# Four interleaved attention layers on one core: another row table for a unit of ten phases, with four shared maxima in place of three, and exp tiles picked by which engine last read the product's bank

## The chip, the cores and the metric

One core of a Trainium2 chip runs the whole kernel. The metric is the device time of one execution in microseconds (us), lower is better. Before the change the median of three runs is 5589.08 us (5588.31 to 5590.57).

## The reference, cut to what matters

Four transformer layers follow each other on `x` of 2048 tokens by 576 channels: attention A, attention B, A again, B again, each with a layer norm ahead and a residual sum behind it. There are 32 heads of 18 channels. In B all heads share one key and one value.

```python
def layer_A(x):                       # x: 2048 x 576, after the layer norm
    q, k, v = split(x @ wqkv)         # 32 heads of 18 channels
    scores = einsum("hqd,hkd->hqk", q, k) * 18 ** -0.5
    p = softmax(scores, axis=-1)
    return einsum("hqk,hkd->hqd", p, v).reshape(2048, 576) @ wo

def layer_B(x):                       # the same, with one k and one v for all heads
    q, k, v = x @ wq, x @ wk, x @ wv
    ...

x = x + layer_A(layernorm(x)); x = x + layer_B(layernorm(x))
x = x + layer_A(layernorm(x)); x = x + layer_B(layernorm(x))
```

## The kernel before, in words

**What a layer does.** It projects q, k and v, then works through 16 pairs of heads (`p`) and four blocks of 512 queries (`u`): 64 units of work in a layer. Head 0 of the pair (`a` = 0) has its rows in partitions 0 to 63 of the `big` tile, head 1 in partitions 64 to 127, so a product of one head uses one half of TensorE's rows.

**What a unit does.** Three kinds of step run interleaved, for different units:

- *Maxima.* 32 steps `m`: a product of 128 queries by 512 keys (`psm`, lines 593), of which VectorE takes the row maximum (`reduce_max`, line 598). With a *shared* maximum, two blocks of keys of the same queries are covered by one step `r` and one step `m`: `r` is the product with the difference of the two key blocks (line 587), of which ScalarE takes the Relu (line 591); the later `m` is the ordinary product of the first block, and VectorE's `tensor_tensor_reduce` (line 596) adds the Relu to it and takes the maximum of the sum. So each `r` puts one more instruction on ScalarE and one less on VectorE.
- *Exponentials.* 32 steps `e` (`exp_mm`): a product of 128 keys by 512 queries (`pse`, line 812), then Exp on ScalarE into an SBUF tile `pt` (line 816). The maxima of that unit were found 14 steps (`LEAD`) earlier, and go through `neg` (line 788), GpSimd, a transpose on VectorE (line 797) and DRAM into rows of `big`.
- *Weighted sums.* `pv_cols` and `pv_block`: four products at a time (line 837) of `pt` tiles with v, into the four column groups of the one bank `oacc`. They lag the exponentials by 928 columns (`PV_LAG`). When a unit is done ScalarE copies `oacc` out as `oc` (line 844), and GpSimd sums and scales it (`o_sum`, `o_mul`).

**What sets the order.** The order is written by hand. The table `UNIT` lists ten phases, each a string of rows and a number of columns. A row is a kind (`m`, `r` or `e`), a head and a rank: `e01` is an exponential of head 0 of rank 1. The loop at the end issues a phase's rows and then as many columns of weighted sums. All engines take their instructions in that order.

**Banks.** PSUM has eight banks: `oacc` and seven that the rows share. `lru` lists the seven by how long ago each was handed out; a row takes the one at its rank (0 is the oldest), so its product waits until ScalarE or VectorE has read what that bank held before.

**Exp tiles.** `ptile` hands out 15 SBUF tiles in turn, for `pt`, `oc` and others. An Exp that writes a tile which ScalarE wrote earlier may need a wait of ScalarE on its own semaphore, where no other wait implies it. `run_todo` issues the small steps of the other units (loads, sums, the path of the maxima) at the start of a phase.

**Names of the phases.** Counted 0 to 9 in table order. A phase's *score part* is the time from its first row's product to its first weighted sum; its *sum part* goes from there to the next phase's first product.

Of the kernel before, what the change touches and what calls it, by code (L numbers as in the profile page):

```python
# [64 lines left out]
UNIT = [("e01 m10 e00 m10 m00 e11", 384),  # L65
        ("m10 e00 m10 e00 e10 m01", 544),
        ("e10 m01 e10 m01 m10 e00", 384),
        ("e10 m00 e10 e00 m10 e01", 352),
        ("m10 m00 e10 m00 e01 r10", 416),
        ("m00 e10 r11 e00 m11 e00 m10", 416),  # L70
        ("m01 e10 e10 e11 m00 e01 m10", 384),
        ("m10 e00 m00 e11 m00 e11", 384),
        ("m00 r10 e00 m01 e10 m01 e10", 416),
        ("m11 e00 e00 m00 e10 e00 m10", 416)]
# [7 lines left out]
def tile_kernel(ctx: ExitStack, tc: tile.TileContext, A_x, A_wqkv, A_wo, B_x, B_wq, B_wk, B_wv, B_wo, out):  # L82
# [65 lines left out]

    lru, turns = list(range(7)), {"m": 0, "e": 0}
# [260 lines left out]
    for layer in range(4):  # L410
# [125 lines left out]
        def ops(p):  # L536
            return big[:, q_slot(p)], big[:, k_slot(p)]
# [35 lines left out]
        def max_mm(bank=mtile):  # L573

            i = m_done[0]
# [5 lines left out]
            mx, ps = mxs[p, u], bank("psm")  # L581
            b, r = 64 * a, 16 * a + 4 * qc + kb
            c0 = u * 512 + qc * P
            if (p, u) >= (0, 2) and (a, qc, kb) in m_diff:
# [5 lines left out]
                t = relus[p, u, a, qc] = relu[:, :512]  # L590
                nc.scalar.activation(t, ps, AF.Relu)  # L591
# [16 lines left out]
        relus, diffs, kd_pair = {}, {}, {}  # L608

# [196 lines left out]
        def exp_mm(p, u, i, rank):  # L806

            a, kc = (i // 2) % 2, i // 4 * 2 + i % 2
            q, k = ops(p)
            e = oldest(rank)("pse")  # L810
            r = 64 * a
            nc.tensor.matmul(e, k[r:r + KE, kc * P:(kc + 1) * P], q[r:r + KE, u * 512:(u + 1) * 512],  # L812
                             start=True, stop=True)

            pt = pts[p, u, i] = ptile("pt")
            nc.scalar.activation(pt, e, AF.Exp, scale=SCALE)  # L816

# [11 lines left out]
        def pv_block(n, c0, c1):  # L829
# [4 lines left out]
            for i in range(i, i + 4) if turn[0] % 2 else range(i + 3, i - 1, -1):  # L834
                a, kc = (i // 2) % 2, i // 4 * 2 + i % 2
                j = 64 * a + 32 * (kc % 2)
                nc.tensor.matmul(oacc[j:j + DH + 1, cs], v_of(kc)[:, 2 * p + a if is_a else 0, :], pts[p, u, i][:, cs],  # L837
                                 start=kc < 2 and c0 == 0, stop=kc >= 14 and c1 == 512)
                if c1 == 512:
                    pts.pop((p, u, i))  # L840
            if c1 == 512 and i // 4 == STEPS - 1:
                oc = ocs[p, u] = ptile("oc")
# [92 lines left out]
        e_next = [0, 0]  # L935

# [65 lines left out]
```

## Time and profile before

| | before |
|---|---|
| time, median of 3 | 5589.08 us |
| the profiled execution: its time, its span | 5593.45 us, 5591.6 us |
| busy share of the span, TensorE / VectorE / ScalarE / GpSimd | 99 / 89 / 87 / 33% |
| TensorE's granted clock | 0.998 |
| rows per layer in the loop over `UNIT` | 1992 of 2048 `m` and `r` |

"PE" is TensorE's products, "PEld" its weight loads, DVE is VectorE, ACT ScalarE, POOL GpSimd, SP the queue that issues DMAs. A row of the timeline reads: start, duration, engine, line, operation, output and input, how many of them in a run. The start and end of an instruction on ACT and DVE overlap with the next one's: their rate is read from one start to the next, not from the duration. Ends of products are modelled, so PE is read by starts as well.

### The profile page before, as it was taken

To read this page: it belongs to the slowest core of one execution; us is meant where nothing else is said; L and a number is where in the kernel's file an instruction comes from. 1 tells how busy PE (TensorE), PEld (TensorE's weight loads), DVE (VectorE), ACT (ScalarE), POOL (GpSimd) and SP (SyncE) were. 2 spreads that over 40 slices of the span, in tenths; PEclk is the share of its full clock that TensorE was granted. 3 is DMA by queue.
4 is the path that set the end of the run, shared out by engine and by line. 5 is a ranking of instruction groups with operands and counts; after the bars stand their busy time and mean duration, and the time that the engine had idled before them with its cause. 6 is when DMAs were issued, how large, how long until landed. Compare 5 with 4: busy or idle time off the path is not lost.

```text
span 5591.6 us, 144494 instructions
## 1 busy us (share of the span) xinstructions
PE 5549.8 (99%) x55774; PEld 3117.2 (56%) x55774; DVE 4999.5 (89%) x9489; ACT 4843.4 (87%) x9624; POOL 1835.7 (33%) x2396
## 2 busy tenths in 40 slices
PE   9999999999999999999999999999999999999999
PEld 8655555554855555555686555555548555555556
DVE  4799999998699999999747999999977999999995
ACT  2599999999389999999725999999992999999996
POOL 3143333334233333333412433333342333333232
PEclk9999999999999999999999999999999999999999
DMA  6421111111421001011243211111114211100102
GB/s 204 127 55 46 42 47 44 45 45 24 131 69 24 24 21 24 21 24 25 61 167 110 59 44 45 43 46 46 40 30 135 58 24 24 24 22 22 23 15 80
DMA packets 275193, 301.73 MB, mean 54 GB/s; under 512 B 135246, under 2 KB 193190, under 8 KB 265214
## 3 DMA queue, kind: packets, MB, share of 16 engines
q1 hardware_dynamic: 274502, 292.49, 18.9%
q8 instruction: 437, 7.16, 0.5%
q14 instruction: 254, 2.08, 0.1%
HBM read 168.50 MB, written 119.86 MB: 52 GB/s over the span
## 4 chain that ended last, share of the span: by engine, by line
PE 95%; POOL 2%; DMA 1%; issue 1%; SPq 1%; DVE 0%; ACT 0%; POOLq 0%; ACTq 0%; DVEq 0%
PE oacc L837 37%; PE psm L593 24%; PE pse L812 21%; PE psn L258 7%; PE psq L432 5%; PE psm L587 1%; PE ps L250 0%; DMA big<-qk_d 0%; POOL big L204 0%; POOL ev L444 0%; DMA raw<-in_B_wq_dram 0%; DMA raw<-in_B_wk_dram 0%; DVE mx L598 0%; DMA big<-m_d 0%; DMA xo<-in_A_x_dram 0%
## 5 line engine op out<-in xcount | busy, mean ns | idle before, releaser
L598 DVE TENSOR_REDUCE mx<-psm 128x1 f32<-128x512 f32 x6704 | 4181.8, 682 | 148.4 <-PE psm L593 90.8
L816 ACT ACTIVATE pt<-pse 128x512 f32<-128x512 f32 x8192 | 4195.7, 614 | 55.2 <-PE pse L812 9.6
L593 PE MATMUL psm<-big 62*128 62x512 f32 x7448 | 2563.9, 440 | 11.6 <-ACT pt L816 8.8
L812 PE MATMUL pse<-big 64*128 64x512 f32 x8192 | 2557.6, 437 | 7.9 <-DMA big<-m_d 5.6
L837 PE MATMUL oacc<-pt,vbuf 128*19 128x384 f32 (+8 forms) x26544 | 1735.9, 368 | 4.3 <-DVE oc L175 3.9
L593 PEld LDWEIGHTS psm<-big 62*128 62x128 f32 x7448 | 1215.7, 185 | 775.7 <-ACT pt L816 368.4
L812 PEld LDWEIGHTS pse<-big 64*128 64x128 f32 x8192 | 1251.6, 185 | 611.0 <-DVE mx L598 420.6
L837 PEld LDWEIGHTS oacc<-pt,vbuf 128*19 128x19 f32 x26544 | 546.5, 98 | 787.6 <-issue 583.8
L175 POOL TENSOR_SCALAR os<-oc 32x512 f32<-32x512 f32 x512 | 313.0, 611 | 1791.8 <-ACT oc L844 1538.6
L863 POOL TENSOR_TENSOR rl<-lt,mone 128x8 f32<-128x8 f32 x256 | 423.1, 1653 | 1141.3 <-DMA lt<-os 1129.1
L837 PE MATMUL oacc<-pt,vy 128*19 128x288 f32 (+3 forms) x8176 | 570.9, 383 | 0.0
L596 DVE CUSTOM_DVE_ANT_0 relu<-psm,relu 128x512 f32<-128x512 f32 x744 | 507.0, 681 | 0.9 <-ACT relu L591 0.9
L591 ACT ACTIVATE relu<-psm 128x512 f32<-128x512 f32 x744 | 445.7, 599 | 38.3 <-PE psm L587 18.5
L440 ACT ACTIVATE ev<-psq 128x512 fp32r<-128x512 f32 (+1 forms) x112 | 66.9, 598 | 328.6 <-PE psq L432 227.1
L876 POOL TENSOR_TENSOR os<-os,rb 96x512 f32<-96x512 f32 x256 | 328.8, 1284 | 29.3 <-DMA rb<-r_d 28.1
L854 POOL TENSOR_TENSOR os<-os,oc 96x512 f32<-96x512 f32 x256 | 325.9, 1273 | 21.3
L258 PE MATMUL psn<-wsm,xx 128*128 128x288 f32 x2240 | 308.0, 296 | 0.0
L258 PEld LDWEIGHTS psn<-wsm,xx 128*128 128x128 f32 x2240 | 298.7, 188 | 12.9 <-issue 10.9
L837 PEld LDWEIGHTS oacc<-pt,vy 128*19 128x19 f32 x8176 | 165.5, 98 | 184.7 <-issue 139.5
L446 DVE TENSOR_TENSOR ev<-psq,ev 128x512 fp32r<-128x512 f32 (+1 forms) x84 | 58.0, 691 | 214.0 <-ACT ev L440 197.5
L432 PE MATMUL psq<-yx,big 128*128 128x512 f32 (+2 forms) x826 | 195.9, 389 | 3.5 <-ACT evr L443 1.8
L432 PE MATMUL psq<-xx,big 128*128 128x512 f32 (+1 forms) x784 | 195.0, 399 | 1.8 <-ACT evr L443 1.8
(93 smaller groups left out, 2229.8 us busy)
## 6 DMA issues: line engine op xcount, KB each, us to landing
big<-qk_d SPq DMA_DIRECT2D x172, 432.0 KB
qk_d<-ev SPq DMA_DIRECT2D x96, 512.0 KB
qk_d<-ev SPq DMA_DIRECT2D x120, 256.0 KB
rb<-r_d SPq DMA_DIRECT2D x512, 36.0 KB
o_d<-os SPq DMA_DIRECT2D x512, 36.0 KB
m_d<-tr SPq DMA_DIRECT2D x1024, 2.0 KB
o<-o_d SPq DMA_DIRECT2D x64, 256.0 KB
xx<-qk_d SPq DMA_DIRECT2D x120, 72.0 KB
```

Source lines behind the costliest of these rows:

```text
L258: nc.tensor.matmul(ps, lhs[:, xc, :], wsm[:, wc, h * 288:(h + 1) * 288], start=i == 0, stop=i == len(TERMS) - 1)
L432: nc.tensor.matmul(ps[:n].rearrange("p (u t) -> p u t", u=2)[:, us], w[:, wc, :n], xts[T][:, us, xc, :], start=(xc, wc) == TERMS[0], stop= ...
L591: nc.scalar.activation(t, ps, AF.Relu)
L593: nc.tensor.matmul(ps, q[b:b + KM, c0:c0 + P], k[b:b + KM, kb * 512:(kb + 1) * 512], start=True, stop=True)
L596: nc.vector.tensor_tensor_reduce(t, ps, t, 1.0, LOWEST, OP.add, OP.max, mx[:, r:r + 1])
L598: nc.vector.reduce_max(mx[:, r:r + 1], ps, axis=AX.X)
L812: nc.tensor.matmul(e, k[r:r + KE, kc * P:(kc + 1) * P], q[r:r + KE, u * 512:(u + 1) * 512], start=True, stop=True)
L816: nc.scalar.activation(pt, e, AF.Exp, scale=SCALE)
L837: nc.tensor.matmul(oacc[j:j + DH + 1, cs], v_of(kc)[:, 2 * p + a if is_a else 0, :], pts[p, u, i][:, cs], start=kc < 2 and c0 == 0, stop=k ...
L854: nc.gpsimd.tensor_tensor(t[:96], t[:96], oc[:96], op=OP.add)
L863: nc.gpsimd.tensor_tensor(rl, lts.pop((p, u)), mone, op=OP.pow)
L876: nc.gpsimd.tensor_tensor(t[:96], t[:96], rb[:96], op=OP.mult)
```

## The change

The table `UNIT` is another one. It has ten phases, 64 rows and 4096 columns as before, with four `r` in place of three, phases of four to seven rows in place of six and seven, and rank 2 in some rows. Two of its ten lines:

```diff
-        ("e10 m00 e10 e00 m10 e01", 352),
+        ("e10 e01 r10 m00", 256),
...
-        ("m11 e00 e00 m00 e10 e00 m10", 416)]
+        ("e00 m10 m00 m12 e00 r11 e00", 416)]
```

The rest of the change concerns which SBUF tile an Exp writes. `reader` notes for each of the seven banks whether ScalarE read it last. The first 14 exp tiles of a layer become a ring; `slot` hands them out again when their last weighted sum has been issued: by the newest writer if the product's bank was last read by ScalarE or if none of the free ones is known to be finished, and otherwise the first free one that is known to be finished (`wrote`, `seen` and `ticks` count ScalarE's writes). From the 1984th exponential on, tiles come in turn again. `oc` is one fixed tile of the 15.

```diff
+    reader = [False] * 7
     lru, turns = list(range(7)), {"m": 0, "e": 0}
...
             mx, ps = mxs[p, u], bank("psm")
+            by_act = reader[lru[-1]]
+            reader[lru[-1]] = False
...
                 t = relus[p, u, a, qc] = relu[:, :512]
+                reader[lru[-1]] = True
+                if not by_act:
+                    seen[0] = max(seen[0], wrote.get("relu", -1))
+                wrote["relu"] = ticks[0]
+                ticks[0] += 1
                 nc.scalar.activation(t, ps, AF.Relu)
...
+        ring, free, wrote, seen, ticks = [], [], {}, [-1], [0]
...
             q, k = ops(p)
+            by_act = reader[lru[rank]]
             e = oldest(rank)("pse")
+            reader[lru[-1]] = True
...
-            pt = pts[p, u, i] = ptile("pt")
+            pt = pts[p, u, i] = slot(by_act)
             nc.scalar.activation(pt, e, AF.Exp, scale=SCALE)
+
+        def slot(by_act):
+            n = sum(e_next)
+            if n >= 1984:
+                return ptile("pt")
+            if len(ring) < 14:
+                ring.append(ptile("pt"))
+                j = len(ring) - 1
+            else:
+                old = [j for j in free if wrote[j] <= seen[0]]
+                j = old[0] if old and not by_act else max(free, key=lambda j: wrote[j])
+                if not by_act:
+                    seen[0] = max(seen[0], wrote[j])
+                free.remove(j)
+            wrote[j] = ticks[0]
+            ticks[0] += 1
+            return ring[j]
...
-                    pts.pop((p, u, i))
+                    pt = pts.pop((p, u, i))
+                    free.extend(j for j, x in enumerate(ring) if x is pt)
             if c1 == 512 and i // 4 == STEPS - 1:
-                oc = ocs[p, u] = ptile("oc")
+                oc = ocs[p, u] = ocs["tile"]
+                ticks[0] += 1
...
         e_next = [0, 0]
+        ocs["tile"] = ptile("oc")
```

The new lines move the numbers: Relu is line 599 after the change, the maximum 606, the shared one 604, `pse` 823, Exp 827, the weighted sum 865 and `oc` 874; the products of `m` are line 601, those of `r` 590.

**What moves on TensorE.** Two phases of a unit in an A layer, before, from the first row of phase 2: `pse` is the product of an `e` row, `psm` that of an `m` (line 593) or an `r` (line 587), `oacc` the weighted sums with their columns.

```order
L812 MATMUL pse<-big 128x512
L593 MATMUL psm<-big 128x512
L812 MATMUL pse<-big 128x512
L593 MATMUL psm<-big 128x512 x2
L812 MATMUL pse<-big 128x512
L837 MATMUL oacc<-pt,vbuf 19x384 x4
L812 MATMUL pse<-big 128x512
L593 MATMUL psm<-big 128x512
L812 MATMUL pse<-big 128x512 x2
L593 MATMUL psm<-big 128x512
L812 MATMUL pse<-big 128x512
L837 MATMUL oacc<-pt,vbuf 19x128 x4
```

The same two phases after the change:

```order
L823 MATMUL pse<-big 128x512
L601 MATMUL psm<-big 128x512
L823 MATMUL pse<-big 128x512
L601 MATMUL psm<-big 128x512
L823 MATMUL pse<-big 128x512
L601 MATMUL psm<-big 128x512
L865 MATMUL oacc<-pt,vbuf 19x320 x4
L823 MATMUL pse<-big 128x512 x2
L590 MATMUL psm<-big 128x512
L601 MATMUL psm<-big 128x512
L865 MATMUL oacc<-pt,vbuf 19x192 x4
L865 MATMUL oacc<-pt,vbuf 19x64 x4
```

Phase 2 has 320 columns behind it in place of 384, and phase 3 four rows and 256 columns in place of six rows and 352; three of its four rows go to ScalarE (two `e` and an `r`), one to VectorE, where there were four and two.

**What moves on ScalarE.** A unit from the copy of `oacc` on, before, with the semaphores that each instruction waits for (`PE` TensorE, `DVE` VectorE, `Pool` GpSimd, `Activation` ScalarE itself):

```order
L844 ACTIVATE oc<-oacc 128x512 [waits PE_49]
L816 ACTIVATE pt<-pse 128x512 [waits PE_49,Activation_49] x2
L816 ACTIVATE pt<-pse 128x512 [waits PE_49] x2
L816 ACTIVATE pt<-pse 128x512 [waits PE_49,Activation_49]
L816 ACTIVATE pt<-pse 128x512 [waits PE_49] x3
L816 ACTIVATE pt<-pse 128x512 [waits PE_49,Activation_49,Pool_49]
L591 ACTIVATE relu<-psm 128x512 [waits DVE_49,PE_49]
L816 ACTIVATE pt<-pse 128x512 [waits PE_49]
L591 ACTIVATE relu<-psm 128x512 [waits PE_49,Activation_49]
L816 ACTIVATE pt<-pse 128x512 [waits PE_49] x9
L591 ACTIVATE relu<-psm 128x512 [waits PE_49]
L816 ACTIVATE pt<-pse 128x512 [waits PE_49] x6
```

After the change, the whole unit:

```order
L874 ACTIVATE oc<-oacc 128x512 [waits PE_49,Pool_49]
L827 ACTIVATE pt<-pse 128x512 [waits PE_49] x5
L599 ACTIVATE relu<-psm 128x512 [waits DVE_49,PE_49]
L827 ACTIVATE pt<-pse 128x512 [waits PE_49] x2
L599 ACTIVATE relu<-psm 128x512 [waits PE_49,Activation_49]
L827 ACTIVATE pt<-pse 128x512 [waits PE_49] x7
L599 ACTIVATE relu<-psm 128x512 [waits DVE_49,PE_49]
L827 ACTIVATE pt<-pse 128x512 [waits PE_49] x10
L599 ACTIVATE relu<-psm 128x512 [waits PE_49]
L827 ACTIVATE pt<-pse 128x512 [waits PE_49]
L827 ACTIVATE pt<-pse 128x512 [waits PE_49,Activation_49]
L827 ACTIVATE pt<-pse 128x512 [waits PE_49] x6
```

There are four Relus in place of three, two waits of ScalarE on itself in a unit in place of some seven, and the wait for GpSimd stands at `oc` in place of one Exp.

More of the change, by code (lines that the diff above doesn't have):

```diff
@@ L60 @@
 TAIL = 2
-UNIT = [("e01 m10 e00 m10 m00 e11", 384),
-        ("m10 e00 m10 e00 e10 m01", 544),
-        ("e10 m01 e10 m01 m10 e00", 384),
-        ("e10 m00 e10 e00 m10 e01", 352),
[L69 to L73, printed above, removed]
-        ("m11 e00 e00 m00 e10 e00 m10", 416)]
+UNIT = [("e00 m10 m02 e10 e01 e10 m00", 448),
[9 rows of a table added]
 UNIT = [([(o[0], int(o[1]), int(o[2])) for o in rows.split()], cols) for rows, cols in UNIT]
```

7 rows, old and new, of the table UNIT are left out of this document.

## The prediction

> **What bounds the kernel now.** I read the page first. Its parts 1, 4 and 5:
>
> ```profile
> PE 5549.8 (99%) x55774; PEld 3117.2 (56%) x55774; DVE 4999.5 (89%) x9489; ACT 4843.4 (87%) x9624; POOL 1835.7 (33%) x2396
> ...
> PE 95%; POOL 2%; DMA 1%; issue 1%; SPq 1%; DVE 0%; ACT 0%; POOLq 0%; ACTq 0%; DVEq 0%
> ...
> L598 DVE TENSOR_REDUCE mx<-psm 128x1 f32<-128x512 f32 x6704 | 4181.8, 682 | 148.4 <-PE psm L593 90.8
> L816 ACT ACTIVATE pt<-pse 128x512 f32<-128x512 f32 x8192 | 4195.7, 614 | 55.2 <-PE pse L812 9.6
> ```
>
> TensorE looks full and carries 95% of the chain, but the ends of its products are modelled, so "99%" does not say that it never waits. The length of a unit comes from the copy of oacc, which ScalarE does once in each; this is its row for 300 to 1060 us, in the first layer:
>
> ```profile
> L844 ACT ACTIVATE oc<-oacc x41: 597/598/600, 316.0 to 1055.9; 128x512 f32<-128x512 f32 x41
> ```
>
> 41 copies are 40 units: (1055.9 - 316.0) / 40 = 18.50 us. The loop over UNIT issues 1992 / 32 = 62.25 units per layer, 249 in all: 249 x 18.50 = 4606 of 5591.6 us. The change touches only these. 0.1 us of a unit is 25 us.
>
> Two neighbouring units, by engine:
>
> ```profile
> 1000.22:1018.71 18.49, 18.49 (x205) 9.47 (x202) 18.08 (x36) 18.25 (x37) 5.75 (x7) 1.00 0.20 55
> 1018.71:1037.20 18.49, 18.49 (x204) 9.43 (x200) 18.01 (x35) 18.11 (x37) 5.75 (x7) 1.00 0.14 36
> ```
>
> The columns are TensorE, its weight loads, VectorE, ScalarE, GpSimd, the clock. Three engines read nearly full, so what each needs without waiting must be read from starts. TensorE's rows, phases 2 and 3, then 6 and the sums of 1:
>
> ```profile
> 1000.22 0.49 PE L812 MATMUL pse<-big 64*128 64x512 f32 x1
> ...
> 1000.56 0.39 PE L812 MATMUL pse<-big 64*128 64x512 f32 x1
> ...
> 1000.80 0.39 PE L812 MATMUL pse<-big 64*128 64x512 f32 x1
> 1001.12 0.84 PE L837 MATMUL oacc<-pt,vbuf 128*19 128x384 f32 x8
> 1001.89 0.49 PE L812 MATMUL pse<-big 64*128 64x512 f32 x1
> ...
> 1002.23 0.41 PE L812 MATMUL pse<-big 64*128 64x512 f32 x2
> 1002.45 0.39 PE L593 MATMUL psm<-big 62*128 62x512 f32 x1
> 1002.50 0.49 PE L812 MATMUL pse<-big 64*128 64x512 f32 x1
> 1002.92 0.79 PE L837 MATMUL oacc<-pt,vbuf 128*19 128x128 f32 x16
> 1003.64 0.50 PE L593 MATMUL psm<-big 62*128 62x512 f32 x2
> ...
> 1007.38 0.50 PE L593 MATMUL psm<-big 62*128 62x512 f32 x1
> ...
> 1008.50 0.84 PE L837 MATMUL oacc<-pt,vbuf 128*19 128x384 f32 x8
> 1009.27 0.50 PE L593 MATMUL psm<-big 62*128 62x512 f32 x1
> ...
> 1017.66 1.11 PE L837 MATMUL oacc<-pt,vy 128*19 128x32 f32 x16
> 1018.71 0.50 PE L812 MATMUL pse<-big 64*128 64x512 f32 x1
> ```
>
> Products of the two heads start together, so six rows alternating between heads take three slots: at 1000.22, 1000.56 and 1000.80, and the sums begin at 1001.12. That score part is 0.90 us, and each slot after the second adds 0.23 (0.24 in the rows). A phase of seven rows has four slots: 1008.50 - 1007.38 = 1.12. The sum part is 1001.89 - 1001.12 = 0.77 us for 384 columns and 1018.71 - 1017.66 = 1.05 for 544, so 1.75 ns a column and 0.10 for the turn: over ten phases 4096 x 0.00175 + 1.0 = 8.17. Phase 3 shows a wait: its last product starts at 1002.50 in place of some 1002.45, the weight load behind it is exposed, and its sums begin 1.03 after its first product, not 0.90.
>
> TensorE's floor before: six phases of three slots and four of four, 6 x 0.90 + 4 x 1.12 + 8.17 = 18.05. The other 0.45 us of the 18.50 are waits for banks.
>
> The other two engines' rates, from starts:
>
> ```profile
> 1007.95 3.54 ACT L816 ACTIVATE pt<-pse 128x512 f32<-128x512 f32 x7
> 1011.64 0.60 ACT L591 ACTIVATE relu<-psm 128x512 f32<-128x512 f32 x1 [0.16 <-PE psm L587]
> ...
> 1010.35 1.14 ACT L816 ACTIVATE pt<-pse 128x512 f32<-128x512 f32 x2
> ```
>
> The Exp at 1010.35 is the sixth of the run from 1007.95: 2.40 / 5 = 0.48 us each. VectorE:
>
> ```profile
> 1015.59 3.08 DVE L598 TENSOR_REDUCE mx<-psm 128x1 f32<-128x512 f32 x5
> ...
> 1017.99 1.28 DVE L598 TENSOR_REDUCE mx<-psm 128x1 f32<-128x512 f32 x2
> ...
> 1007.27 0.68 DVE L596 CUSTOM_DVE_ANT_0 relu<-psm,relu 128x512 f32<-128x512 f32 x1
> 1007.88 0.08 DVE L596 DVE_READ_ACCUMULATOR2_ANT mx<- 128x1 f32 x1
> 1007.91 1.29 DVE L598 TENSOR_REDUCE mx<-psm 128x1 f32<-128x512 f32 x2
> ...
> 1003.19 0.17 DVE L788 TENSOR_REDUCE neg<-mx 128x8 f32<-128x32 f32 x1
> 1003.28 0.68 DVE L598 TENSOR_REDUCE mx<-psm 128x1 f32<-128x512 f32 x1
> 1004.18 1.89 DVE L598 TENSOR_REDUCE mx<-psm 128x1 f32<-128x512 f32 x3 [0.21 <-PE psm L593]
> 1005.98 0.20 DVE L797 STREAM_TRANSPOSE tr<-hl 128x32 f32<-128x32 f32 x1
> 1006.11 0.65 DVE L598 TENSOR_REDUCE mx<-psm 128x1 f32<-128x512 f32 x1
> ```
>
> The maximum at 1017.99 is the fifth of that run: 2.40 / 4 = 0.60 each. A shared one takes 1007.91 - 1007.27 = 0.64, neg and the transpose 0.09 and 0.13 = 0.22 in a unit. VectorE before: 26 x 0.60 + 3 x 0.64 + 0.22 = 17.74. ScalarE: 32 Exp, 3 Relu, one copy, 36 x 0.48 = 17.28. So TensorE is the longest, VectorE 0.3 behind it, and with seven banks between them they delay each other.
>
> **The change part by part.** *One more shared maximum.* It takes a pass of 0.60 off VectorE, makes another 0.04 longer, and puts 0.48 on ScalarE: VectorE 24 x 0.60 + 4 x 0.64 + 0.22 = 17.18, ScalarE 37 x 0.48 = 17.76. TensorE still makes 64 products. ScalarE: Activation LUTs, Rules for kernel authors, in the Trainium skill, would put a relu or a maximum on VectorE, not on ScalarE; here the rows are 0.48 against 0.60 us, so the trace does not bear that out. By that page's figures (186 ns and 0.833 a column, 93 overlapped) an ACTIVATE of 512 columns takes an estimated 0.52, ScalarE 37 x 0.52 = 19.2 a unit and the kernel some 180 us more; the rows' 0.48 decides.
>
> *The phases.* Rows alternate between heads well enough that six still take three slots and seven four. Now six phases have seven rows, three have six, one has four: 6 x 1.12 + 3 x 0.90 + 0.67 (0.90 less a slot) = 10.09, against 9.88: one slot more, since an odd row takes a slot alone. The columns are 4096 again: 8.17. TensorE's floor rises from 18.05 to 18.26, +0.21.
>
> *The waits.* Here is the gain, if there is one. Before, a phase of three slots and 384 columns lasts 0.90 + 0.77 = 1.67 us and gives VectorE three maxima, 1.80: over by 0.13, in phases 0, 2 and 7; phase 3 lasts 1.62 and gives ScalarE four Exps, 1.92: over by 0.30, and there the trace shows the wait. Now phases 5 to 9 and 0 have seven rows, four for ScalarE (1.92) and three for VectorE (1.80), and last 1.12 + 0.10 + 416 x 0.00175 = 1.95 (2.00 with 448 columns). Phases 1 and 4 last 0.90 + 0.94 = 1.84 with 1.44 and 1.80. Phase 2 lasts 0.90 + 0.66 = 1.56, phase 3 0.67 + 0.55 = 1.22: there VectorE has 1.80 and then one maximum and neg, 0.69, so 2.49 in 2.78.
>
> I followed the banks there row by row. From a phase's first product to its reader takes 0.57 on ScalarE (before, line 587 at 1011.07, Relu at 1011.64) and 0.54 on VectorE (1003.64 to 1004.18); the second product's row stands above, the first's is
>
> ```profile
> 1011.07 0.50 PE L587 MATMUL psm<-xx,big 54*128 54x512 f32 x1
> ```
>
> ScalarE is through phase 1's three Exps at 0.57 + 3 x 0.48 = 2.01, 0.17 into phase 2; it starts the copy there and phase 2's Exps at 0.65, 1.13 and 1.61, and is free at 2.09, when phase 3's first Exp can hardly begin (1.56 + 0.57 = 2.13): no lag is carried on. Phase 3's `m00` needs the bank of the second of those Exps, free at 1.13 + 0.61 = 1.74, and wants it at 1.56 + 0.34 = 1.90. The closest one is phase 6's `m11`: it wants the bank of phase 5's last Exp in its third slot, at 2.00 + 0.58 = 2.58; that Exp starts at 0.57 + 3 x 0.48 = 2.01 and ends at 2.62, so the row waits 0.04 and perhaps for its weight load, beside the seventh row's slot. So I find little wait, but many margins of 0.05 or less. Bounds for the rest: zero, and the 0.45 of before. I take 0.10, near the low end because the walk finds nearly nothing: 18.26 + 0.10 = 18.36.
>
> *The exp tiles.* Waits of ScalarE on itself fall from seven to two a unit. Bound: between nothing and all idle time ahead of the Exps in part 5, 55.2 us, and a slot of 0.48 kept with or without such a wait; I take nothing, since ScalarE is not the longest. The cover is its slack of 18.36 - 17.76 = 0.60. The copy now waits for GpSimd's sum of the last unit's `oc`:
>
> ```profile
> L175 POOL TENSOR_SCALAR os<-oc 32x512 f32<-32x512 f32 x512 | 313.0, 611 | 1791.8 <-ACT oc L844 1538.6
> ...
> L854 POOL TENSOR_TENSOR os<-os,oc 96x512 f32<-96x512 f32 x256 | 325.9, 1273 | 21.3
> ```
>
> Two of 0.61 and one of 1.27 us follow a copy, 2.5 us, and the next copy is 18 us off. The move of `neg`'s and the transpose's rows by two phases shifts the DMA path by less than 4 us of the 14-step lead.
>
> *The sum.* 18.36 - 18.50 = -0.14 us in 249 units: -35 us. The profiled execution, 5593.45 with 1.85 outside its span, would be 5558; on the median of 5589.08, 4.4 lower, **5554 us**.
>
> **The rivals.** *ScalarE becomes the bound (slower).* Six phases in a row give it 1.92 of 1.95 us. If its instructions come at 0.50 there, as with the short idles in
>
> ```profile
> 1000.87 4.62 ACT L816 ACTIVATE pt<-pse 128x512 f32<-128x512 f32 x9
> ```
>
> ((4.62 - 0.60) / 8 = 0.50), each such phase takes 2.00, six times 0.05 = 0.30 more: 18.66, +0.16, 5589 + 40 = 5629 us. It decides from 1.95 / 4 = 0.49. In full, one more instruction on a ScalarE that cannot take it, +0.48, gives 5589 + 120 = 5709. For it: ScalarE's 18.25 busy of 18.49, the highest after TensorE. Against it: durations overlap, and 0.48 holds where no product is late. Perfetto Trace Analysis, Identifying the Most-Contended Engine, in the Trainium skill, counts ScalarE by occupancy and would make it the engine to relieve, so it speaks against loading it; the starts in this trace do not agree. Chance 0.20.
>
> *The slot eats it (no change).* Half of the old waiting stays, 0.24, and 18.26 + 0.24 = 18.50: within 11 us of 5589. For it: rank 2 takes banks read only five rows ago. Chance 0.17.
>
> *VectorE was the bound all along.* Then the unit shrinks with it by 0.56, to 17.94: -139, 5450 us. For it: it is idle only 0.4 of 18.49. The same section of the Trainium skill's Perfetto Trace Analysis discounts matmul busy time and looks to the weight loads, 9.47 of 18.49 here, so by it TensorE would not be the limit. Against it: the starts of the sum parts, spaced alike wherever no bank is late, put TensorE's own floor at 18.05. Chance 0.03.
>
> That the table does nothing is excluded: ScalarE's order shows four Relus a unit.
>
> **How the numbers follow.** The forecast, 5554, has 0.60; with no waits at all it is 18.26, -60, 5529, and its upper end is where the next case begins, 5578. The range reaches over no change and a part of the ScalarE case: 5526 to 5610, leaving out the VectorE case and the worse half of the ScalarE case. About 0.2% (11 us) is what a measurement here tells from no change. Faster 0.63, same 0.17, slower 0.20.
>
> **What would show it.** A unit of 18.3 to 18.4 by the copy's starts; score parts of 1.12 to 1.17 in the seven-row phases and 0.67 to 0.75 in phase 3; ScalarE's starts at 0.48 in phases 5 to 9; VectorE with idle time of over 0.9 a unit. Wrong if a seven-row phase lasts 2.00 or more with ScalarE's reads ending last ahead of its rows, or if phases 2 to 4 wait for VectorE.

## The result and the profile after

The changed kernel takes 5557.59 us, the median of five runs (5554.74 to 5560.95); the kernel before took 5589.96 beside it (5588.31 to 5591.12, five runs). The ratio is 0.9943, interval 0.9932 to 0.9954: 32 us faster, where 35 were forecast.

The page of the profiled execution (5554.74 us, span 5553.0), parts 1, 4 and 5:

```profile
PE 5519.8 (99%) x55774; PEld 3110.0 (56%) x55774; DVE 4949.8 (89%) x9489; ACT 4883.1 (88%) x9872; POOL 1836.8 (33%) x2396
...
PE 96%; POOL 1%; issue 1%; DMA 1%; DVE 0%; SPq 0%; ACT 0%; POOLq 0%; ACTq 0%; DVEq 0%
...
L827 ACT ACTIVATE pt<-pse 128x512 f32<-128x512 f32 x8192 | 4182.4, 614 | 23.1 <-PE pse L823 11.7
L606 DVE TENSOR_REDUCE mx<-psm 128x1 f32<-128x512 f32 x6208 | 3959.1, 685 | 119.8 <-PE psm L601 77.2
...
L599 ACT ACTIVATE relu<-psm 128x512 f32<-128x512 f32 x992 | 622.2, 627 | 0.2
```

Almost nothing here tells the two kernels apart: the shares of busy time are those of before, with 248 Relus and shared maxima more and 496 plain maxima less. Idle time ahead of the Exps fell from 55.2 to 23.1 us, ahead of the maxima from 148.4 to 119.8. The gain shows in the length of a unit, which is again read from the starts of the copy of `oacc`, in the timeline of its line from 300 to 1060 us:

```profile
L874 ACT ACTIVATE oc<-oacc x41: 597/598/607, 316.7 to 1051.3; 128x512 f32<-128x512 f32 x41
```

(1051.3 - 316.7) / 40 = 18.365 us, where it was 18.50, and 249 x 0.135 = 34 us. TensorE's rows for phases 2 and 3, for phase 6, and for phases 9 and 0:

```profile
885.84 0.50 PE L823 MATMUL pse<-big 64*128 64x512 f32 x1
...
886.74 0.73 PE L865 MATMUL oacc<-pt,vbuf 128*19 128x320 f32 x8
887.40 0.51 PE L823 MATMUL pse<-big 64*128 64x512 f32 x2
...
888.08 0.63 PE L865 MATMUL oacc<-pt,vbuf 128*19 128x192 f32 x16
888.64 0.73 PE L601 MATMUL psm<-big 62*128 62x512 f32 x3
...
892.49 0.49 PE L823 MATMUL pse<-big 64*128 64x512 f32 x1
...
893.17 0.50 PE L601 MATMUL psm<-big 62*128 62x512 f32 x2
893.60 0.90 PE L865 MATMUL oacc<-pt,vbuf 128*19 128x32 f32 x16
...
898.36 0.49 PE L823 MATMUL pse<-big 64*128 64x512 f32 x1
...
899.49 0.90 PE L865 MATMUL oacc<-pt,vy 128*19 128x320 f32 x16
900.32 0.50 PE L823 MATMUL pse<-big 64*128 64x512 f32 x1
...
901.45 0.90 PE L865 MATMUL oacc<-pt,vy 128*19 128x416 f32 x8
```

The score parts are 0.90 (886.74 - 885.84), 0.68, 1.11, 1.13 and 1.13; a sum part of 416 columns is 0.83 (900.32 - 899.49). Read in this way and averaged over the 16 units between 700 and 1000 us, the score parts of the ten phases are, in us:

| phase | 0 | 1 | 2 | 3 | 4 | 5 | 6 | 7 | 8 | 9 |
|---|---|---|---|---|---|---|---|---|---|---|
| before | .930 | .927 | .899 | 1.060 | .903 | 1.175 | 1.126 | 1.013 | 1.131 | 1.153 |
| after | 1.132 | .921 | .903 | .683 | .909 | 1.124 | 1.126 | 1.124 | 1.133 | 1.134 |

Against floors of 0.90 for three slots and 1.12 for four, before has 0.44 us too much (phase 3 has 0.16 of it, phase 7 0.11, phase 5 0.055) and after, with 0.67 for phase 3, 0.10. No phase stands out any more. ScalarE's timeline after, through phases 5 to 9 of another unit:

```profile
1001.25 3.54 ACT L827 ACTIVATE pt<-pse 128x512 f32<-128x512 f32 x7
...
1005.16 5.02 ACT L827 ACTIVATE pt<-pse 128x512 f32<-128x512 f32 x10
```

(5.02 - 0.60) / 9 = 0.49 a start. On the mean of the units between 700 and 1000 us, the first Exp of phases 6 to 9 starts 0.51 to 0.52 behind its predecessor, since it waits a little for its product, the one behind it 0.493, and the others 0.477. ScalarE follows TensorE and has little to spare. VectorE, at 0.60 us a maximum, 0.64 a shared one and 0.22 for the rest, is idle for 18.365 - 17.18 = 1.19 us of a unit, 18.50 - 17.74 = 0.76 before.

### The profile page after: what moved, and what is told of

The parts are those of the page before. It is cut to its first block, busy times and chain, and to the rows that moved or that the text cites. A ratio compares the mean times of both kernels' runs of the same rounds, so it can differ in the third digit from the quotient of the medians.

```text
span 5553.0 us, 143953 instructions
## 1 busy us (share of the span) xinstructions
PE 5519.8 (99%) x55774; PEld 3110.0 (56%) x55774; DVE 4949.8 (89%) x9489; ACT 4883.1 (88%) x9872; POOL 1836.8 (33%) x2396
## 4 chain that ended last, share of the span: by engine, by line
PE 96%; POOL 1%; issue 1%; DMA 1%; DVE 0%; SPq 0%; ACT 0%; POOLq 0%; ACTq 0%; DVEq 0%
PE oacc L865 37%; PE pse L823 27%; PE psm L601 17%; PE psn L259 7%; PE psq L433 5%; PE psm L590 3%; PE ps L251 0%; DMA big<-qk_d 0%; POOL ev L445 0%; ACT pt L827 0%; DVE mx L606 0%; DMA xo<-in_A_x_dram 0%; DMA raw<-in_B_wk_dram 0%; DMA xx<-qk_d 0%; DMA big<-m_d 0%
## 5 line engine op out<-in xcount | busy, mean ns | idle before, releaser
L827 ACT ACTIVATE pt<-pse 128x512 f32<-128x512 f32 x8192 | 4182.4, 614 | 23.1 <-PE pse L823 11.7
L606 DVE TENSOR_REDUCE mx<-psm 128x1 f32<-128x512 f32 x6208 | 3959.1, 685 | 119.8 <-PE psm L601 77.2
L823 PE MATMUL pse<-big 64*128 64x512 f32 x8192 | 2288.2, 433 | 3.2 <-DMA big<-m_d 1.9
L601 PE MATMUL psm<-big 62*128 62x512 f32 x7200 | 2194.9, 443 | 7.9 <-DVE mx L604 4.3
L823 PEld LDWEIGHTS pse<-big 64*128 64x128 f32 x8192 | 1177.1, 185 | 1071.6 <-ACT pt L827 742.3
L865 PE MATMUL oacc<-pt,vbuf 128*19 128x32 f32 (+11 forms) x26544 | 1731.6, 368 | 4.0 <-DVE oc L176 4.0
L601 PEld LDWEIGHTS psm<-big 62*128 62x128 f32 x7200 | 913.1, 184 | 172.7 <-ACT pt L827 33.9
L604 DVE CUSTOM_DVE_ANT_0 relu<-psm,relu 128x512 f32<-128x512 f32 x992 | 686.1, 692 | 32.6 <-PE pse L823 1.1
L599 ACT ACTIVATE relu<-psm 128x512 f32<-128x512 f32 x992 | 622.2, 627 | 0.2
L590 PE MATMUL psm<-big 54*128 54x512 f32 x512 | 215.1, 420 | 0.0
L590 PE MATMUL psm<-xx,big 54*128 54x512 f32 x480 | 201.2, 419 | 0.0
```

The lines of the kernel that those rows point to most:

```text
L590: nc.tensor.matmul(ps.rearrange("p (h t) -> p h t", h=2) if p == 0 or not is_a else ps, q[b:b + 3 * DH, c0:c0 + P], k, start=True, stop=True)
L601: nc.tensor.matmul(ps, q[b:b + KM, c0:c0 + P], k[b:b + KM, kb * 512:(kb + 1) * 512], start=True, stop=True)
L604: nc.vector.tensor_tensor_reduce(t, ps, t, 1.0, LOWEST, OP.add, OP.max, mx[:, r:r + 1])
L606: nc.vector.reduce_max(mx[:, r:r + 1], ps, axis=AX.X)
```

## The experiments

The theory was that a unit is TensorE's floor, set by the slots of each phase and the columns, plus waits for banks that vanish when each phase is as long as what it gives to its slower reader, and that the exp tiles add nothing. The rivals were that the tiles carry a part of the gain, that ScalarE sets the length, and that the slots cost nothing. Each kernel ran beside the kernel before; ratios are to that. The times and what they mean, in short:

| kernel | us | ratio (interval) | unit, us |
|---|---|---|---|
| the change | 5557.59 | 0.9943 (0.9932 to 0.9954) | 18.37 |
| 1 new table only | 5574.72 | 0.9976 (0.9966 to 0.9986) | 18.44 |
| 2 tile rule only | 5595.73 | 1.0014 (1.0005 to 1.0023) | 18.54 |
| 3 table, fixed copy tile | 5565.47 | 0.9956 (0.9942 to 0.9970) | 18.39 |
| 4 columns moved | 5592.71 | 1.0009 (1.0000 to 1.0018) | 18.52 |
| 5 `r11` to `m11` | 5716.03 | 1.0229 (1.0215 to 1.0243) | 19.03 |
| 6 the same, another bank | 5661.16 | 1.0130 (1.0117 to 1.0144) | 18.80 |
| 7 `m01` to `r01` | 5729.74 | 1.0257 (1.0243 to 1.0271) | 19.11 |
| 8 other rows in phase 8 | 5632.74 | 1.0082 (1.0068 to 1.0096) | 18.68 |
| 9 other heads in phase 7 | 5586.97 | 0.9999 (0.9990 to 1.0007) | 18.50 |
| 10 five rows of one head | 5613.12 | 1.0043 (1.0030 to 1.0057) | 18.59 |
| 11 phases of six rows | 5703.66 | 1.0207 (1.0193 to 1.0221) | 18.98 |
| 12 a quarter fewer sums | 5498.51 | 0.9842 (0.9828 to 0.9855) | 18.13 |

**1. The new table only** (the kernel before, with the ten lines of the new `UNIT`; the tiles in turn as before).

```diff
-UNIT = [("e01 m10 e00 m10 m00 e11", 384),
...
-        ("m11 e00 e00 m00 e10 e00 m10", 416)]
+UNIT = [("e00 m10 m02 e10 e01 e10 m00", 448),
...
+        ("e00 m10 m00 m12 e00 r11 e00", 416)]
```

> The kernel before with the new row table alone; exp tiles and the copy's tile go in turn as before. Theory (the phases carry the gain; ScalarE is 0.6 us a unit shorter than TensorE, so its waits on itself cost nothing): 5557 us, within 8 of the changed kernel, a unit of 18.36 to 18.39 us. Rival (the order of the tiles carries a good part): 5570 us or more, a unit of 18.42 or more, with the missing time in phases whose first Exp waits on ScalarE itself.

The table alone brings 0.24%, some 13 us, and not all of the gain, as the theory had it. Time and unit are where the rival put them, but the larger part of the loss is a wait for GpSimd, not for ScalarE itself. Eight phases are within 0.007 us of the change; phase 6 has a score part of 1.172 (after: 1.126) and phase 3 one of 0.707 (after: 0.683). TensorE's rows in a phase 6, in this kernel:

```profile
894.82 0.50 PE L812 MATMUL pse<-big 64*128 64x512 f32 x1
...
895.57 0.50 PE L593 MATMUL psm<-big 62*128 62x512 f32 x2
896.00 0.90 PE L837 MATMUL oacc<-pt,vbuf 128*19 128x32 f32 x16
```

`m11` starts 0.75 after the phase's first product and the sums 1.18 after it; in the change it was 0.68 and 1.11. That is the row which the prediction named as the closest one: it waits for phase 5's last Exp. ScalarE's timeline, from the Relu of phase 4 to the first Exp of phase 5, shows that Exp late:

```profile
726.82 0.62 ACT L591 ACTIVATE relu<-psm 128x512 f32<-128x512 f32 x1
727.52 3.54 ACT L816 ACTIVATE pt<-pse 128x512 f32<-128x512 f32 x7
```

The distance is 0.70. This Exp waits for two engines, TensorE and GpSimd. In the timeline of the Exp's line from 724 to 730 us, the last of these three separate wait instructions, at 727.46, is the one for its product; the Exp behind it holds the wait for GpSimd, which had ended its last work on the copy at 725.84:

```profile
L816 ACTq EVENT_SEMAPHORE  x3: 17/17/17, 724.3 to 727.5; - x3
```

**2. The tile rule only** (the change, with the ten old lines of `UNIT`).

```diff
-UNIT = [("e00 m10 m02 e10 e01 e10 m00", 448),
...
-        ("e00 m10 m00 m12 e00 r11 e00", 416)]
+UNIT = [("e01 m10 e00 m10 m00 e11", 384),
...
+        ("m11 e00 e00 m00 e10 e00 m10", 416)]
```

> The changed kernel with the old row table; exp tiles by the last reader of the bank, one fixed tile for the copy. Theory: the old table's 0.45 us of waiting in a unit comes from its phases, so 5589 us, within 8 of the kernel before, a unit of 18.47 to 18.52. Rival (the tiles carry a good part): under 5575 us.

With the old rows the tile rule gains nothing; the kernel is even slower by 0.14%, a little beyond what was expected (9 us above the kernel before, a unit of 18.54), with phases 1 (0.948) and 3 (1.089) each 0.02 to 0.03 longer than before. So the 0.33% between the new table (0.9976) and the whole change (0.9943), some 18 us, belong to the two together.

The traces show where phases 1 and 3 grow. In the kernel before, every second unit has a second wait, of ScalarE on itself, both at the Exp that opens phase 0 and at the copy. In those units phase 1 has 0.94 to 0.97 us and phase 3 1.08 to 1.10, in the others 0.90 and 1.01 to 1.04 (17 units between 690 and 1010 us). With the tile rule all 17 units have a second wait at both places, now for GpSimd at the copy, and all are of the longer kind.

**3. The table with a fixed tile for the copy** (kernel 1, and `oc` in a tile of its own, so that the wait for GpSimd stands at the copy; the exp tiles in turn over the other 14).

```diff
-        return pool.tile(list(shape), dt, tag="p", bufs=15, name=name)
+        return pool.tile(list(shape), dt, tag="p", bufs=14, name=name)
+
+    oc_tile = cst.tile([P, 512], F32, name="oc")
...
-                oc = ocs[p, u] = ptile("oc")
+                oc = ocs[p, u] = ocs["tile"]
...
+        ocs["tile"] = oc_tile
```

> The kernel before with the new row table and one fixed tile for the copy of oacc; exp tiles in turn over the other 14. In the run with the table alone a unit is 18.44 us in place of 18.37: phase 6's score part is 1.17 in place of 1.13, and the first Exp of phase 5, which there also waits for GpSimd, comes 0.06 later after the one ahead of it. Theory (that wait, moved onto the copy by the fixed tile, is most of what the tiles are worth): phase 6 back to 1.13, a unit of 18.37 to 18.39, 5557 to 5563 us. Rival (ScalarE's waits on itself, which the ring takes away, are what counts): 5572 us or more, phase 6 at 1.17 still.

The time is just above what was expected, and its interval touches both kernel 1's and the change's; the phases tell more. Phase 6 is back at 1.128, and the Relu of phase 4 and the Exp behind it are 0.64 apart:

```profile
724.23 0.62 ACT L593 ACTIVATE relu<-psm 128x512 f32<-128x512 f32 x1
724.87 3.54 ACT L818 ACTIVATE pt<-pse 128x512 f32<-128x512 f32 x7
```

This is the change's distance (725.10 to 725.75 there). So moving one wait from an Exp that opens a full phase to the copy is worth 0.044 us of the 0.07 that the unit loses without the tile rule, 11 us. Phase 3 stays at 0.708: the other 0.025, some 6 us, goes with the ring itself. Every second unit is late there. Here are two neighbours, each from the first product of phase 1, with the first Exp of phase 1 and the first product and first sum of phase 3:

```profile
736.16 0.49 PE L595 MATMUL psm<-big 62*128 62x512 f32 x1
736.78 0.60 ACT L818 ACTIVATE pt<-pse 128x512 f32<-128x512 f32 x1
739.57 0.49 PE L814 MATMUL pse<-big 64*128 64x512 f32 x2
740.31 0.63 PE L839 MATMUL oacc<-pt,vbuf 128*19 128x192 f32 x16
...
754.58 0.49 PE L595 MATMUL psm<-big 62*128 62x512 f32 x1
755.14 0.60 ACT L818 ACTIVATE pt<-pse 128x512 f32<-128x512 f32 x1
757.99 0.50 PE L814 MATMUL pse<-big 64*128 64x512 f32 x2
758.68 0.52 PE L839 MATMUL oacc<-pt,vbuf 128*19 128x192 f32 x8
```

In the first unit the Exp has a second wait, of ScalarE on itself, and starts 0.62 after phase 1's first product; in the second it has none and starts after 0.56. Phase 3's score parts are 0.74 and 0.69. Kernels 1 and 3 have 34 such units between 690 and 1010 us: the 17 with this wait have 0.72 to 0.74, the 17 without 0.67 to 0.70, and the change never has the wait. From there to phase 2's second Exp, whose bank phase 3's `m00` takes, ScalarE has no gap to make it up. So here too the cost is a second wait at an Exp that opens a phase. This is read from the traces; no kernel moves this wait alone. Most other waits of ScalarE on itself cost nothing that shows: kernel 1 has six in a unit, the change two.

**4. Columns moved between two phases that are alike.** Phases 7 and 8 have the same rows and banks; nothing but the place of 96 columns of sums changes.

```diff
-        ("e10 m00 e10 e02 e10 m01 m10", 416),
-        ("e10 m00 e10 e02 e10 m01 m10", 416),
+        ("e10 m00 e10 e02 e10 m01 m10", 320),
+        ("e10 m00 e10 e02 e10 m01 m10", 512),
```

> The changed kernel with 96 columns of weighted sums moved from phase 7 (320 in place of 416) to phase 8 (512): all totals of rows, columns and slots are the same. Theory (each phase must be as long as what it gives ScalarE and VectorE): phase 7 lasts 1.12 + 0.66 = 1.78 us against ScalarE's 1.92, so its rows or those of phase 8 wait some 0.13 us in all, +32, 5590 us (5575 to 5605). Rival (only the totals of a unit count, seven banks even out a phase): 5558 us, within 8.

Met: +0.66% on the change. TensorE's rows of phase 8:

```profile
901.73 0.50 PE L823 MATMUL pse<-big 64*128 64x512 f32 x1
...
902.55 0.54 PE L601 MATMUL psm<-big 62*128 62x512 f32 x2
903.02 1.06 PE L865 MATMUL oacc<-pt,vy 128*19 128x320 f32 x16
904.01 0.50 PE L823 MATMUL pse<-big 64*128 64x512 f32 x1
```

The score part is 1.29 where it was 1.13, and every other phase is unchanged. The phase ahead lasts 1.79 us in place of 1.95, too short for the four Exps that it gives away (4 x 0.48 = 1.92), and the next phase's rows paid for that; the 0.16 us that phase 8 got more of afterwards bought nothing. Work and floor are the same in sum, so this is the local balance by itself.

**5. The fourth shared maximum taken back**, and **6.** the same with an exponential of phase 0 on another bank.

```diff
-        ("e00 m10 m00 m12 e00 r11 e00", 416)]
+        ("e00 m10 m00 m12 e00 m11 e00", 416)]
```

```diff
-UNIT = [("e00 m10 m02 e10 e01 e10 m00", 448),
+UNIT = [("e00 m10 m02 e10 e02 e10 m00", 448),
```

> The changed kernel with phase 9's r11 made an m11: three shared maxima in a unit, as before the change, the phases and slots as after. Theory (TensorE's floor of 18.26 stands, and a phase must hold what it gives the readers): phase 9 gives VectorE four maxima, 2.40 us in 1.96, and VectorE needs 17.74 of the unit; it makes up 0.15 a phase afterwards, so some 0.1 to 0.4 us of waits in phases 9, 0 and 1: 5582 to 5655 us, likeliest 5600. Rival (VectorE has room to spare, the fourth shared maximum only loads ScalarE): 5558 us or less.

> The run with three shared maxima in the new table, with phase 0's e01 made e02. In that run nearly all of the loss, 0.67 us a unit, stood in phase 0, where e01 took the bank of phase 9's fourth maximum. Theory (the price is one row on a bank that is read last, and rank 2 takes a bank of ScalarE's that is free by then): phase 0's wait falls by 0.3 to 0.6, since m00, the seventh row, then takes that bank 0.23 later; a unit of 18.45 to 18.75 in place of 19.03, 5578 to 5650 us. Rival (VectorE's total of 17.74 us a unit costs it, wherever the bank): within 15 of 5716 us.

The direction of kernel 5 was right, its size not: 2.9% more than the change, above the expected range. The whole loss stands in phase 0, whose score part is 1.81 in place of 1.13:

```profile
885.54 0.50 PE L823 MATMUL pse<-big 64*128 64x512 f32 x1
...
886.68 0.51 PE L823 MATMUL pse<-big 64*128 64x512 f32 x2 [0.40 <-DVE mx L606]
887.03 0.40 PE L601 MATMUL psm<-big 62*128 62x512 f32 x1
887.35 0.95 PE L865 MATMUL oacc<-pt,vy 128*19 128x416 f32 x16
```

TensorE stands still for 0.40 us for a maximum. Phase 9 now gives VectorE four rows, and the rank-1 row in phase 0 takes just the bank that VectorE reads last. With rank 2 in kernel 6 the phase falls to 1.57, a third of the loss less: in the expected direction, not quite as far as expected (5661 us, where 5650 was the most), and it still waits. So the fourth shared maximum pays through the place where it stands, not only by VectorE's total.

**7. A fifth shared maximum.**

```diff
-        ("e10 m00 e10 e02 e10 m01 m10", 416),
+        ("e10 m00 e10 e02 e10 r01 m10", 416),
```

> The changed kernel with phase 8's m01 made an r01: five shared maxima. ScalarE needs 38 x 0.48 = 18.24 us of a unit, VectorE 16.6, TensorE's floor is 18.26 as before. Theory: phase 8 gives ScalarE five, 2.40 us in 1.96, and phases 9 and 0 have no room to make it up, so the rows of phases 9, 0 and 1 wait 0.2 to 0.5 us: 5605 to 5680 us, likeliest 5630. Rival (VectorE set the pace): 5545 us or less. Rival (ScalarE has its 0.6 us of slack anywhere in the unit): 5558.

Again the direction held and the expected size was too small: five rows of phase 8 go to ScalarE, 2.4 us of work in 1.96, and phase 9's score part is 1.852 in place of 1.134. Everything else is the same to 0.015 us. TensorE's rows of phase 9:

```profile
881.76 0.50 PE L823 MATMUL pse<-big 64*128 64x512 f32 x1
881.76 0.72 PE L601 MATMUL psm<-big 62*128 62x512 f32 x2
882.95 0.50 PE L601 MATMUL psm<-big 62*128 62x512 f32 x1 [0.46 <-ACT relu L599]
882.95 0.73 PE L823 MATMUL pse<-big 64*128 64x512 f32 x2
```

The row at 882.95 is `m12`, of head 1: it takes the bank of the new `r01`, the last of the five. The `e00` of head 0 behind it starts with it, though the Exp that read its bank before had ended at 881.92.

**8. Other rows in phase 8**, four of head 1 as before, ordered so that three of them come first.

```diff
-        ("e10 m00 e10 e02 e10 m01 m10", 416),
+        ("e10 e10 e10 m00 e02 m01 m10", 416),
```

> The changed kernel with the rows of phase 8 in the order e10 e10 e10 m00 e02 m01 m10: the same work on every engine, but the heads do not alternate, so the phase takes five slots of TensorE in place of four. Theory (TensorE's slots set the unit): phase 8's score part grows from 1.13 by 0.23 to some 1.36 us, a unit from 18.37 to 18.60, 249 units: +57, 5615 us. Rival (ScalarE or VectorE sets the unit, and TensorE only waits for them): the slot takes the place of a wait, under 5570 us.

This was to cost a slot and missed: phase 8 has 0.175 more and phase 9 0.134, together 5632.74 us. Head 1 still has four products and the phase still four slots. The waits come from the banks, which the new order hands out otherwise: in phase 8 `e02` waits for VectorE until 0.64 us after the phase's first product, and head 0's next row follows 0.34 later. It doesn't measure a slot.

**9. Other heads in phase 7.**

```diff
-        ("e10 m00 e10 e02 e10 m01 m10", 416),
+        ("e10 m10 e10 e02 e10 m01 m00", 416),
```

> The changed kernel with the heads of phase 7's two maxima of rank 0 exchanged (e10 m10 e10 e02 e10 m01 m00): every engine has the same kinds of work in the same order, but phase 7 takes five slots of TensorE in place of four. Theory (TensorE's slots set the unit): +0.23 in phase 7, a unit of 18.60, +57, 5615 us (5600 to 5625). Rival (ScalarE, whose rows ran at 18.13 a unit when TensorE had a quarter of its sums less, sets the unit): the slot is half hidden or more, 5585 us or less.

The phase grew by 0.137, not by a slot; the time, 5587 us, lies between the theory's and the rival's. In program order the rows are `pse`, `psm`, `pse`, `pse`, `pse`, `psm`, `psm`, the fourth being head 0's `e02`. TensorE's timeline:

```profile
879.80 0.51 PE L823 MATMUL pse<-big 64*128 64x512 f32 x2
880.13 0.40 PE L601 MATMUL psm<-big 62*128 62x512 f32 x1
880.38 0.40 PE L823 MATMUL pse<-big 64*128 64x512 f32 x1
880.39 0.50 PE L601 MATMUL psm<-big 62*128 62x512 f32 x1
880.61 0.39 PE L823 MATMUL pse<-big 64*128 64x512 f32 x1
880.73 0.39 PE L601 MATMUL psm<-big 62*128 62x512 f32 x1
```

Two `pse` start together at 879.80, ahead of the second and the third row, which share a half of TensorE's rows with the first: the second of them can only be `e02`. (Its weight load waits for VectorE, and of the phase's `pse` rows only `e02` takes a bank that VectorE read last.) So a row that waits only for its half does not hold up the rows of the other head, and the phase has the four slots of head 1 (879.80, 880.13, 880.38, 880.61). Head 0 ends it: its `m01` starts at 880.39, late for its bank, and `m00` 0.34 behind it, where rows that follow without a wait are 0.23 apart.

**10. Five rows of one head in phase 7**, with three in phase 8: the kinds and banks stay, two rows change heads.

```diff
-        ("e10 m00 e10 e02 e10 m01 m10", 416),
-        ("e10 m00 e10 e02 e10 m01 m10", 416),
+        ("e10 m00 e10 e02 e10 m11 m10", 416),
+        ("e10 m00 e10 e02 e10 m01 m00", 416),
```

> The changed kernel with phase 7's m01 made m11 and phase 8's m10 made m00: as many rows of each head in a unit, the same order of work on ScalarE and VectorE, but phase 7 has five products of head 1 and two of head 0. The run with exchanged heads in phase 7 showed that a product of the other head starts ahead of earlier rows, so that a phase is as long as the head with more rows, and not as the row order; there that was still four. Theory (TensorE's longest head sets a phase): +0.23 in phase 7, a unit of 18.60 in place of 18.37, +57, 5614 us (5600 to 5625). Rival (ScalarE, at 18.13 a unit, or VectorE sets the pace and TensorE's slot is hidden): 5580 us or less.

Met. Phase 7's score part is 1.358 on the mean, 0.234 more, and all others are as in the change; one of them in TensorE's timeline:

```profile
881.20 0.49 PE L823 MATMUL pse<-big 64*128 64x512 f32 x1
...
881.54 0.62 PE L823 MATMUL pse<-big 64*128 64x512 f32 x3
882.00 0.64 PE L601 MATMUL psm<-big 62*128 62x512 f32 x2
882.57 0.41 PE L865 MATMUL oacc<-pt,vbuf 128*19 128x128 f32 x8
```

A slot costs 0.23 us of a unit, 56 us of the kernel: here what TensorE has more to do shows in full.

**11. Phases of six rows**: the same rows, kinds and banks in phases 3 to 6, cut six and six, which has one slot less in a unit than the change.

```diff
-        ("e10 e01 r10 m00", 256),
-        ("m00 m10 m00 e10 e02 r10", 480),
-        ("m10 e00 m12 m00 e11 e01 e10", 448),
-        ("e01 m10 e02 e10 r01 m11 m00", 416),
+        ("e10 e01 r10 m00 m00 m10", 352),
+        ("m00 e10 e02 r10 m10 e00", 448),
+        ("m12 m00 e11 e01 e10 e01", 416),
+        ("m10 e02 e10 r01 m11 m00", 384),
```

> The changed kernel with the same 64 rows in the same order and banks, cut into phases differently: phases 3 to 6 have six rows each (352, 448, 416, 384 columns) in place of 4, 6, 7 and 7, so a unit has 34 slots and TensorE's floor falls from 18.26 to 18.03. Theory: phases 4 and 5 give ScalarE four, 1.92 us, in 1.78 and 1.73, so it falls 0.33 behind there, and what the slot saves comes back as waits: a unit of 18.3 to 18.5, 5540 to 5590 us, likeliest 5562. Rival (only TensorE's floor counts): 18.13, 5500 us.

Missed by far: 2.7% above the change. The floor is lower by a slot, and the waits grow by some 0.83 us: phase 3 has 1.175, phase 5 1.324, phase 7 1.250 and phase 8 1.170 us of score part. By their floors phases 4 and 5 last 1.78 and 1.73 us, and each gives ScalarE four rows, 1.92. Phase 3's 0.275 stands ahead of them and was not in the theory: its new last row, `m10`, waits for the last Exp of phase 2; in the change that row comes only behind phase 3's sums. The unequal table with one slot more beats this equal one with fewer.

**12. A quarter fewer weighted sums**, to take work off TensorE alone; columns 384 to 511 of every step are left out, and the lag is shortened with them.

```diff
-PV_LAG = 928
+PV_LAG = 696
...
+    nc.vector.memset(oacc[:, 384:], 1.0)
...
-                n, c0 = divmod(pv_at[0], 512)
-                w = min(cols, 512 - c0)
+                n, c0 = divmod(pv_at[0], 384)
+                w = min(cols, 384 - c0)
...
+            cols = cols * 3 // 4
```

> The changed kernel with a quarter of the weighted sums left out (columns 384 to 511 of every step, and all columns of the table times 0.75): TensorE's floor falls from 18.26 to 10.09 + 6.38 = 16.47 us a unit, ScalarE's 17.76 and VectorE's 17.18 stay. Theory (TensorE is the longest by 0.5, ScalarE is next): the unit falls to between 17.76 and 18.1, 249 units and some: 5408 to 5490 us, likeliest 5450, with ScalarE's starts 0.48 apart nearly throughout. Rival (the readers set the unit, TensorE's sums lie in their shadow): 5540 us or more.

By 1.75 ns a column TensorE has 1.79 us less to do in a unit; the unit falls by 0.23, to 18.13, a little less than expected (18.1 at most, 5490 us). The row of the windows from 700 to 1000 us (length, then the busy time and count of TensorE, its weight loads, VectorE, ScalarE, GpSimd; the clock) for this kernel:

```profile
700.00:1000.00 300.00, 299.89 (x3318) 163.92 (x3310) 292.83 (x564) 299.98 (x614) 109.59 (x137) 1.00 0.18 46
```

TensorE's score parts are longer than in the change by 1.47 us in all, in every phase but one: it now waits for banks. ScalarE is busy for 299.98 of 300 us, and 18.13 / 37 = 0.490 a start. With these phases the readers hold the unit some 0.23 us below the change, not 0.60. That ScalarE alone does so is not shown: 68% of its starts are 0.48 behind the last (51% in the change), and at that rate throughout it would need 17.76.

## Why the prediction was right, and where it was wrong

*The unit.* Forecast 18.36, measured 18.365; -35 us against -32. The working holds in its terms too: TensorE's floor of 18.26 (one slot more, 0.21) plus waits of 0.10. The sum parts, averaged over the same units, add up to 8.18 (8.17 taken), and the score parts lie 0.10 above their floors. That a slot has its full price was shown by kernel 10, at 0.234 with everything else unchanged.

*The waits.* "Here is the gain, if there is one": that phases are matched to what they give their readers was shown by kernel 4, which changes nothing else and loses 0.15 us, more than the 0.135 gained. Kernels 5, 7 and 11 show the same from the side of the rows. They break the new table, and each loses more than it gained; how much of the gain comes from the columns, from the fourth shared maximum and from the ranks, no kernel here separates. The excess of phase 3 before, 0.16, was the largest, as its balance said, though some 0.03 of it goes with ScalarE's second waits (kernel 2); that of phase 2, put at 0.13 short, did not exist (0.899), so the balance finds candidates and does not size them.

*The exp tiles.* "I take nothing, since ScalarE is not the longest" is the step that failed. They are worth some 18 of the 32 us with the new table, and nothing with the old one. The cover named, ScalarE's slack of 0.60 in a unit, is that of an engine over ten phases; what decides is the margin of one row at one place, and the walk had that row: phase 6's `m11`, late by 0.04. 0.06 us more ahead of the Exp that opens phase 5 is passed on to it through four Exps without a gap, since nothing in the phase has slack for it (kernel 1, and its undoing in kernel 3). In every second unit of kernels 1 and 3 the Exp that opens phase 1 does the same to phase 3. The total came out right because the waits, taken as 0.10, were those with these second waits gone; the prediction did not see that the table alone would not reach them, and that the two met is in part luck.

*ScalarE.* Its slack was too large as well: 37 x 0.48 = 17.76 counts distances within a phase, but the first Exp of a phase is 0.51 to 0.52 behind, and no run here brought a unit below 18.13. The rival that ScalarE becomes the bound did not come true, but its point of decision, 0.49 a start, was reached on the mean: it was nearer than its chance was argued from.

*The slots.* Their number was right and the reason wrong: "an odd row takes a slot alone", counted along the program order, is not how they form. Where no bank is late, the two heads run as two streams, and a phase has as many slots as the head with more rows (kernels 9 and 10). TensorE then does not start its products in the order of issue, as was said of all engines ahead of the prediction. Alternating rows give the same count, so the sum did not suffer; kernel 8, built on the wrong reason, did.

*What would show it.* Score parts of 1.12 to 1.13 in the phases of seven rows and 0.683 in phase 3, and a unit of 18.36, came as named. ScalarE's starts are 0.477 within a phase but 0.49 on the mean. VectorE's idle time is 1.19 by starts, over the 0.9 named, and only (300.00 - 291.97) / 16.3 = 0.49 by busy time, in which its durations overlap:

```profile
700.00:1000.00 300.00, 300.00 (x3270) 154.03 (x3266) 291.97 (x557) 299.67 (x605) 108.08 (x137) 1.00 0.18 46
```

The same row has ScalarE busy for 299.67 of 300 and TensorE's weight loads for 154.03, a little over half. Perfetto Trace Analysis, Identifying the Most-Contended Engine, in the Trainium skill, which judges ScalarE by occupancy and TensorE, beside its share of peak arithmetic, by its weight loads, would point to ScalarE as the engine that sets the time. Kernel 10 is against it: a slot more on TensorE, with ScalarE's instructions the same, cost 0.23 us of 0.23.

*What stays open.* What holds the unit at 18.13 in kernel 12, and how the table's own part is shared out between its columns, its fourth shared maximum and its ranks. That ScalarE's second wait at the Exp that opens phase 1 costs phase 3's 0.025 us, some 6 of the 32, rests on the traces of kernels 1 and 3 alone.

## What to carry to other kernels

Where several engines are nearly full and pass banks to each other in a fixed order, the time is set stretch by stretch: make each stretch of the leading engine as long as the work that it hands to its slowest reader, even at the cost of a higher floor. Count the margin of a small wait at the row that follows from it, not by the slack of its engine over the whole loop; the same wait costs nothing at one instruction and 11 us at another. And undo each part of a change alone and add each alone: here one part is worth less than half of the gain, the other nothing, and the two together all of it.

## What the runs showed of the hardware that was not expected

- Products of the two halves of TensorE's rows run as two streams while they wait only for their half: in kernel 9 the fourth product in program order starts with the first, ahead of the second and third. TensorE: Matmul & The Clock Gate, The mechanism (its Part 3), in the Trainium skill, has products start strictly in program order; the rows at 879.80 to 880.61 differ from that. A product that waits for a bank does hold up the other half: in kernel 7 the `e00` of head 0 starts at 882.95 with the `m12` ahead of it, 1.03 us after its own bank was read.
- A row of a head that comes after a wait for a bank is followed by the next 0.34 us later, where it is 0.23 in an unbroken run (kernel 9): there the wait cost 0.11 us beyond itself. Kernel 7 has the same 0.34 behind its wait at 882.95, kernel 8 behind that of `e02`. The first two rows of a phase are 0.33 apart as well.
- An Exp that opens a phase starts about 0.06 us later with a second wait than without: 0.70 against 0.64 behind its predecessor where the wait is for GpSimd, and in another phase 0.576 in the change, where it is for ScalarE itself, against 0.513 in kernel 3 without it (means of 16 units). That is with the wait long fulfilled for GpSimd, by 1.6 us in kernel 1. The instruction for the wait itself is shown with 17 ns.
- One row given to the other reader in one phase costs 0.66 to 0.74 us of a unit (kernels 5 and 7), more than the row's own 0.48 or 0.60. In kernel 5 a third of that came from the bank that the waiting row takes (kernel 6).
